# Pooled attention and a bilinear layer on one core: p times v for both heads per 128 queries, on two column halves of the array

## The chip, the core and the metric

The kernel runs on one core of one Trainium2 chip. Five engines work side by side, each with its own queue that it works off in order: TensorE (PE in the profile; its weight loads are listed apart as PEld), VectorE (DVE), ScalarE (ACT), GpSimd (POOL), and SyncE (SP), which here only issues DMAs. They wait for each other through semaphores. The metric is the device time of one execution in microseconds (us); the median of the runs counts.

## What is computed

```python
# attention: batch 4, heads 8, keys 1152, head dimension 64
q_pool = q.reshape(B, H, S // 2, 2, D).mean(axis=3)            # 576 queries
scores = scale * np.matmul(q_pool, k.transpose(0, 1, 3, 2))
scores = scores - np.max(scores, axis=-1, keepdims=True)
attn = np.exp(scores)
attn = attn / (np.sum(attn, axis=-1, keepdims=True) + 1e-09)
x = np.matmul(attn, v)                                         # 4 x 8 x 576 x 64
# bilinear layer on the 2304 tokens (512 wide, 1536 inside)
a = x @ w_a
b = x @ w_b
out = a * b @ w_out
```

Inputs and outputs are float32. To keep that precision with float16 products the kernel splits p, v, x and the weights w_a and w_b (and, from the second batch on, k and q) into a high and a low float16 part; a product is then three products: high times high, high times low, low times high.

## The kernel before, in words

**Attention.** Two heads form a pair; there are 16 pairs, four to a batch. A pair's 576 queries are worked in rows of 128 queries: two rows make the "even" token group (256 tokens), two the "odd" group (256), and 64 queries are the "rest". A block is 128 queries of one head, or the rest's 64 queries of both heads: nine blocks a pair, 144 in all. A block passes through: scores on PE into the PSUM tile `sps` (`qk`, and `qk_rest` for what didn't fit); the minimum of the negated scores on DVE (`sm_max`, L566), which also moves them to `s`; exp on ACT (L573); sum and reciprocal on DVE; the high part p on ACT (`sm_hi`, L586) and the low part on DVE (`sm_lo`, L590); and one DMA that transposes both parts into a slot of `pt` (`transpose`, L596, issued by SP).

**p times v.** `unit` (before) handles one head and all 256 or 320 queries of a token group at once, in the one PSUM bank `xps`. `pv` does it in two parts: nine matmuls (L622) whose weights are 128 columns, v's high and low part side by side, so that the upper 64 partitions collect v_hi p_hi and the lower 64 v_lo p_hi; then ten matmuls (L632) with v_hi alone (64 columns) and p_lo, which go in turn to the upper and the lower half. The two halves are then added on the way out: `x_copy` on ACT (L641) copies the upper half, `x_add` on DVE (L647) adds the lower. A pair takes four units and five of each of these. For each head the slots of `pt` that a unit reads must lie side by side, so each block has a fixed slot out of six.

**Weights and the bilinear layer.** The weights arrive as 64-bit pairs, 36 pieces of 512 KB; each is loaded into one of four `raw` buffers, in turn, and split there by ACT, DVE and POOL. The buffers are borrowed: two lie in `xt`, two in the lines 4 to 11 of `g`. The bilinear layer works in nine tiles of 256 tokens: `moe_mm` (L722, 288 matmuls a tile), `moe_a` on ACT and `moe_g` on DVE, and `moe_o` (L748, 72 matmuls a tile). Tile 0 needs the even tokens of all four pairs of batch 0 and the weights; the tiles 6, 8 and 7, which come last, need the last pair.

**What sets the order.** Every step is a task with a duration in us, a priority key and its buffers (`add`). The class `Plan` simulates the queues with the table `LAT` (latency from engine to engine), the DMA constants and PE's clock, tries 20 priority orders, and emits the best. So each number in the table or in an `add` can move any instruction on any queue. Once emitted, each engine's order is fixed.

Of the kernel before, what the change touches and what calls it, by code (L numbers as in the profile page):

```python
# [19 lines left out]
NQ = S // 2  # L20
# [10 lines left out]
A0, R0, REMN = (0, 64, 64, 64), (256, 0, 0, 0), 64  # L31
# [11 lines left out]
    (0.02, 0.29, 0.29, 0.29, 0.29),  # L43
    (0.3, 0.13, 0.14, 0.17, 0.17),
    (0.2, 0.14, 0.15, 0.17, 0.17),
    (0.15, 0.15, 0.15, 0.15, 0.15),
    (0.1, 0.0, 0.0, 0.0, 1.05),
)
SEED, TRIALS, SWEEPS = 3, 20, 3
DMA_START, DMA_END = 0.72, 0.97  # L50
Z_ALL = 30
W_KEY = (-3, 1.3)
W_PASSES = 4
PE_TICK, PE_WARM = 3.413, 1.275


class Plan:
# [9 lines left out]
    def add(self, eng, dur, key, fn, args=(), r=(), w=(), gen=0.45, block=0.0, port=None, lag=0.0, after=()):  # L67
# [14 lines left out]
        self.tasks.append((ENGINES.index(eng), dur, key, fn, args, sorted(deps), gen, block, eng == "POOL" if port is None else port, lag))  # L82
        return n

    def run(self, key, back):

        eng, dur, lat, out, left, gen, block, port, lag = self.back if back else self.forth
# [5 lines left out]
        dma_free = port_free = 0.0  # L93
        busy = {}
# [6 lines left out]
        for _ in range(n):  # L101
# [54 lines left out]
    def order(self):  # L156
        n = len(self.tasks)
        eng, dur, key, _, _, deps, gen, block, port, lag = map(list, zip(*self.tasks))
# [5 lines left out]
        self.forth = (eng, dur, LAT, out, [len(x) for x in deps], gen, block, port, lag)  # L164
        self.back = (eng, dur, back, deps, [len(x) for x in out], gen, [0.0] * n, port, lag)
# [22 lines left out]
def kernel(  # L188
# [53 lines left out]
    def PT(name, shape):  # L242
# [4 lines left out]
    xps = PT("xps", [128, 512])  # L247
    acc = [x.rearrange("p a n -> p (a n)") for x in ab]
# [8 lines left out]
        g_t[:, 4 * j:4 * j + 4].rearrange("p f n -> p (f n)").bitcast(I32).rearrange("p (n w) -> p n w", w=2)  # L257
        for j in (1, 2)
# [3 lines left out]
    z_t += [wab[:, NF - 1, m].rearrange("p a c n -> p (a c n)").bitcast(F32) for m in range(2)]  # L262

# [30 lines left out]
    def k_sum():  # L294

        nc.tensor.matmul(xps[:, 0:2], one.broadcast_to([128, 128]), kmx, start=True, stop=True)

    def k_scale(u):
        inv = ksc[:, u, 2:4]
        nc.vector.tensor_scalar(  # L300
            out=inv, in0=xps[:, 0:2], scalar1=2.0 ** -100, scalar2=2.0 ** -14, op0=ALU.max, op1=ALU.mult
# [30 lines left out]
    def prep_qk(ps_, key):  # L332
        n = ps_.q1 - ps_.q0
        if ps_.split:
            u = f"ksc{ps_.u}"
            add("SP", 2.5, key - 3, load_k, (ps_.p, 0), w=["kn0"])
            add("SP", 2.5 * n / NQ, key - 3, load_q, (ps_.p, ps_.q0, ps_.q1), w=["qraw"])
            add("POOL", 0.1 + 1.55 * n / NQ, key, q_sum, (0, n), r=["qraw"], w=["qs0"])
            add("DVE", 1.35, key, k_max, (), r=["kn0"], w=["kmx0"])
            add("DVE", 0.1 + 0.6 * n / NQ, key, q_max, (n,), r=["qs0"], w=["kmx1"])  # L340
            add("PE", 0.45, key - 2, k_sum, (), r=["kmx0", "kmx1", "ones"], w=["xps"])
            add("DVE", 0.7, key - 2, k_scale, (ps_.u,), r=["xps"], w=[u])
            return
# [154 lines left out]
    def prep_w(f, key):  # L498
        for m in range(3):
# [4 lines left out]
            if m < 2:  # L504
                add("DVE", 0.74, key, w_max, (f, m, n), w=[z, f"wmx{f}{m}"])
# [447 lines left out]
```

## Time and profile before

| | |
|---|---|
| median of 3 runs | 935.23 us (935.16 to 935.75) |
| profiled execution, its own time | 939.15 us |
| its span (first to last instruction) | 937.4 us |
| mean granted TensorE clock | 0.922 |
| PE, DVE, ACT, POOL busy | 85%, 76%, 64%, 28% of the span |
| DMA | 141.4 MB, 151 GB/s in the mean |

All rows come from the profiled execution. Shares of busy time are means over stages that differ much: the first sixth, in which the weights are prepared, a long middle, in which attention and the bilinear layer run side by side, and the last 170 us, in which only the bilinear layer is left. So the rows below are cut by stretch where that matters. A PE that is shown busy may run at either of two clock levels (granted clock 1.00 is 2.4 GHz, 0.50 is 1.2 GHz).

### The profile page before, as it was taken

The numbers are of one execution on the slowest core, as the hardware profiler recorded it, in microseconds if no ns is written. First come the engines' busy times: TensorE is split into PE (matmuls) and PEld (weight loads), VectorE is DVE, ScalarE is ACT, GpSimd is POOL, SyncE is SP. The second block draws the span as 40 slices with busy tenths as digits, with TensorE's granted clock in tenths as the row PEclk, the third lists the DMA queues.
The fourth block names the chain that finished last, engine by engine and source line by source line (L and its number), as shares of the span: only waits on it lengthen the run. The fifth ranks groups of instructions, "written<-read, shape, count | busy, mean of one in ns | idle before, by whom it ended". The sixth has DMA issues, their size and how long they took to land.

```text
span 937.4 us, 15587 instructions
## 1 busy us (share of the span) xinstructions
PE 792.7 (85%) x5856; PEld 562.4 (60%) x5856; DVE 710.0 (76%) x1352; ACT 600.6 (64%) x973; POOL 265.0 (28%) x228
## 2 busy tenths in 40 slices
PE   4546436998789988669999999899999998999997
PEld 2323224665456755337766776576677666877885
DVE  6699999996799889998999799989889873112010
ACT  5677977966577768857787687667867762232212
POOL 4547687622311012111023113201310231110303
PEclk9666667999789999969999999999999999999999
DMA  7999799886989889987878979979786674000100
GB/s 254 235 205 243 201 236 221 222 188 121 198 174 157 155 164 195 206 167 146 174 156 167 176 152 161 199 130 175 150 162 141 103 151 76 1 23 2 23 1 23
DMA packets 353644, 141.40 MB, mean 151 GB/s; under 512 B 338208, under 2 KB 340256, under 8 KB 353568
## 3 DMA queue, kind: packets, MB, share of 16 engines
q1 hardware_dynamic: 353568, 140.40, 71.5%
q8 instruction: 46, 0.75, 0.3%
q14 instruction: 30, 0.25, 0.1%
HBM read 50.72 MB, written 4.72 MB: 59 GB/s over the span
## 4 chain that ended last, share of the span: by engine, by line
PE 50%; DVE 8%; issue 3%; DMA 2%; ACT 2%; POOL 0%; ACTq 0%; DVEq 0%
PE ab L722 24%; PE ab L748 12%; PE sps L538 7%; PE xps L622 4%; DVE p L590 2%; PE xps L632 2%; DVE s L566 2%; DMA pt<-p 2%; ACT p L586 1%; ACT g L729 0%; DVE k L315 0%; DVE x L647 0%; DVE g L734 0%; DVE o L754 0%; ACT s L573 0%
## 5 line engine op out<-in xcount | busy, mean ns | idle before, releaser
L722 PEld LDWEIGHTS <-wab 128*128 128x128 f16 x2592 | 248.9, 98 | 42.6 <-issue 6.2
L722 PE MATMUL ab<-xt,wab 128*128 128x256 f16 x2304 | 267.0, 274 | 2.8 <-DVE o L754 1.6
L590 DVE SCALAR_TENSOR_TENSOR p<-s,st,p 128x1152 f16<-128x1152 f32 x144 | 212.8, 1484 | 9.9 <-ACT p L586 9.6
L573 ACT ACTIVATE s<-s,st 128x1152 f32<-128x1152 f32 x144 | 179.9, 1250 | 56.3 <-DVE s L566 55.4
L586 ACT ACTIVATE p<-s,st 128x1152 f16<-128x1152 f32 x144 | 178.2, 1245 | 22.1 <-DMA pt<-p 7.8
L742 POOL TENSOR_TENSOR gl<-g,gh 128x256 fp32r<-128x256 f32 x108 | 95.9, 892 | 308.6 <-ACT gh L739 299.2
L566 DVE TENSOR_SCALAR_CACHE_REDUCE s<-sps,ksc 128x1152 f32<-128x1152 f32 x108 | 152.8, 1414 | 20.6 <-PE sps L538 18.5
L748 PE MATMUL ab<-wo,gh 128*128 128x512 f32 x432 | 144.4, 416 | 4.9 <-DVE g L734 4.9
L538 PE MATMUL sps<-k,q 64*128 64x512 f16 (+3 forms) x1080 | 122.0, 339 | 29.9 <-DVE s L566 25.1
L729 ACT ACTIVATE g<-ab,cc 128x256 f32<-128x256 f32 (+1 forms) x144 | 56.0, 417 | 106.0 <-PE ab L722 105.7
L622 PE MATMUL xps<-pt,vs 128*128 128x256 f16 (+1 forms) x576 | 91.4, 310 | 37.0 <-DMA pt<-p 17.2
L538 PEld LDWEIGHTS <-q 64*128 64x128 f16 (+1 forms) x1080 | 58.6, 99 | 102.9 <-issue 63.2
L734 DVE SCALAR_TENSOR_TENSOR g<-ab,cc,g 128x256 f32<-128x256 f32 (+1 forms) x144 | 56.2, 412 | 75.3 <-ACT g L729 74.7
L535 PE MATMUL sps<-k,q 64*128 64x512 f32 (+3 forms) x240 | 71.4, 675 | 41.5 <-DVE s L566 33.4
L622 PEld LDWEIGHTS <-vs 128*128 128x128 f16 x576 | 58.3, 106 | 59.9 <-issue 39.4
L748 PEld LDWEIGHTS ab<-wo,gh 128*128 128x128 f32 x432 | 78.0, 192 | 26.5 <-DVE g L734 2.6
L748 PE MATMUL ab<-wo,gl 128*128 128x512 f32 x216 | 86.7, 402 | 0.0
L535 PEld LDWEIGHTS sps<-k,q 64*128 64x128 f32 (+1 forms) x240 | 33.2, 236 | 79.1 <-DVE s L566 37.0
L739 ACT ACTIVATE gh<-g 128x256 fp32r<-128x256 f32 x108 | 43.9, 411 | 52.0 <-PE ab L748 50.9
L286 POOL TENSOR_TENSOR q<-qraw 128x576 f32<-128x576 f32 (+2 forms) x20 | 30.6, 1532 | 134.6 <-DVE q L323 42.0
L641 ACT ACTIVATE x<-xps 64x256 f32<-64x256 f32 (+2 forms) x80 | 28.1, 351 | 59.6 <-PE xps L632 54.9
L566 DVE TENSOR_SCALAR_CACHE_REDUCE s<-sps 128x1152 f32<-128x1152 f32 x36 | 48.7, 1353 | 9.1 <-PE sps L535 8.6
(88 smaller groups left out, 812.1 us busy)
## 6 DMA issues: line engine op xcount, KB each, us to landing
vraw<-in_v_dram SPq DMA_DIRECT2D x19, 576.0 KB, 4.5
k<-in_k_dram SPq DMA_DIRECT2D x19, 576.0 KB, 4.7
qraw<-in_q_dram SPq DMA_DIRECT2D x12, 576.0 KB, 5.0
g<-in_w_ab_dram SPq DMA_DIRECT2D x12, 512.0 KB, 4.5
xt<-in_w_ab_dram SPq DMA_DIRECT2D x12, 512.0 KB, 4.5
out_dram<-o SPq DMA_DIRECT2D x16, 256.0 KB, 2.8
g<-in_w_out_dram SPq DMA_DIRECT2D x6, 512.0 KB, 4.8
xt<-in_w_out_dram SPq DMA_DIRECT2D x6, 512.0 KB, 4.3
```

The source lines that it names most:

```text
L535: nc.tensor.matmul(out, qs[jq][rows, queries], kn[jk][rows, keys], start=True, stop=True)
L538: nc.tensor.matmul(out, qf[rows, hq - 1, queries], kf[rows, hk - 1, keys], start=(hq, hk) == (1, 1), stop=(hq, hk) == (2, 1),)
L566: nc.vector.tensor_scalar(out=s_t[sbuf(i)], in0=sps[:, at:at + S], scalar1=-1.0 / 16.0 if u is None else ksc[:, u, 4:5], scalar2=None, op0 ...
L573: nc.scalar.activation(out=s, in_=s, func=AF.Exp, scale=-1.0, bias=t[:, 0:1], accum_out=t[:, 1:2])
L586: nc.scalar.activation(out=p_t[pbuf(i)][:, 0], in_=s_t[sbuf(i)], func=AF.Copy, scale=st_t[i % NST][:, 3:4])
L590: nc.vector.scalar_tensor_tensor(out=p[:, 1], in0=s, scalar=st_t[i % NST][:, 3:4], in1=p[:, 0], op0=ALU.mult, op1=ALU.subtract)
L622: nc.tensor.matmul(xps[:, 0:w], vs[:, c, e].rearrange("p a d -> p (a d)"), pt[:, 0, c, c0:c0 + w], start=(c == 0), stop=False,)
L722: nc.tensor.matmul(dst if t < 8 else dst.rearrange("p (b n) -> p b n", b=B), wab[:, f, 1 - m, a, c], moe_x(t, b, c), start=(n == 0), stop= ...
L729: nc.scalar.activation(out=g_t[:, f, c], in_=ab[j][:, 1, c], func=AF.Copy, scale=cc[:, b, f, 0:1])
L734: nc.vector.scalar_tensor_tensor(out=g, in0=ab[j][:, 0, c], scalar=cc[:, b, f, 1:2], in1=g, op0=ALU.mult, op1=ALU.mult)
L742: nc.gpsimd.tensor_tensor(out=gl_t[j], in0=g_t[:, f], in1=gh_t[j].bitcast(F32), op=ALU.subtract)
L748: nc.tensor.matmul(acc[u], g[:, us], wo[:, f, a], start=(first and n == 0), stop=(last and n == 2))
```

## The change

- `unit` now handles both heads of one row of 128 (or 64) queries. `pv` (L634 after) makes, for each of nine key chunks, three pairs of matmuls with 64-column weights: head 0 to the upper 64 partitions of `xps`, head 1 to the lower 64. That is 54 matmuls a unit and five units a pair. All three products of a head add up in the same place, so nothing has to be added afterwards: `x_add` is gone.
- Units of one token group write neighbouring columns of `xps`; one `x_copy` over 128 partitions (`leave`) then takes out the whole group. The small column sums (`sums`) move to the last two columns of the same bank.
- The slots of `pt` are used in turn by all blocks.
- The queries stand in the same order in every batch (`A0`, `R0` are gone).
- Two of the four `raw` buffers change places: the one in `g` lines 4 to 7 goes, and one in `wab`'s slab 10 is borrowed until piece 30; after that only the two in `xt` are used.
- Nearly all figures of the planner change (durations, latencies, DMA constants), and it gets a price for changing the kind of matmul (`PE_TURN`). So the whole order is planned anew.

```diff
-A0, R0, REMN = (0, 64, 64, 64), (256, 0, 0, 0), 64
+REMN = 64
...
-    (0.02, 0.29, 0.29, 0.29, 0.29),
...
+    (0.0, 0.22, 0.13, 0.3, 0.3),
...
-DMA_START, DMA_END = 0.72, 0.97
-Z_ALL = 30
-W_KEY = (-3, 1.3)
+DMA_START, DMA_END, LOAD_LAG = 0.72, 0.63, 0.8
+Z_ALL, R_ALL = 30, 30
+W_KEY = (4, 1.3)
 W_PASSES = 4
-PE_TICK, PE_WARM = 3.413, 1.275
+PE_TICK, PE_WARM, PE_TURN = 3.413, 1.275, 0.1
...
                 if e == PE:
+                    if mode[i] != last:
+                        d += PE_TURN
+                        last = mode[i]
+                    end = t + d
...
+    sums = xps[:, 510:512]
...
-        g_t[:, 4 * j:4 * j + 4].rearrange("p f n -> p (f n)").bitcast(I32).rearrange("p (n w) -> p n w", w=2)
-        for j in (1, 2)
+        x.bitcast(I32).rearrange("p (n w) -> p n w", w=2)
+        for x in (wab[:, NF - 2].rearrange("p m a c n -> p (m a c n)"), g_t[:, 8:12].rearrange("p f n -> p (f n)"))
...
+    def ri(n):
+        return n % NRAW if n < R_ALL else n % 2
...
-        nc.tensor.matmul(xps[:, 0:2], one.broadcast_to([128, 128]), kmx, start=True, stop=True)
+        nc.tensor.matmul(sums, one.broadcast_to([128, 128]), kmx, start=True, stop=True)
...
+            last += ["raw2"] if f == NF - 2 and m < 2 else []
...
-            add("PE", 1.55 if ps_.split else 1.93, i - 8, qk, (ps_, rows, ps_.jk, ps_.jq), r=r, w=["sps0", "sps1"])
+            add("PE", 1.52 if ps_.split else 1.92, i - 8, qk, (ps_, rows, ps_.jk, ps_.jq), r=r, w=["sps0", "sps1"], mode=1)
         else:
-            add("PE", 0.18 if ps_.split else 0.24, i - 9, qk_rest, (ps_, rows, ps_.jk, ps_.jq), r=r, w=["sps1"],
-                after=(ps_.last_max,))
+            add("PE", 0.19 if ps_.split else 0.26, i - 9, qk_rest, (ps_, rows, ps_.jk, ps_.jq), r=r, w=["sps1"],
+                after=(ps_.last_max,), mode=1)
...
-        add("SP", 2.75, i, transpose, (i,), r=[p + "h", p + "l"], w=[f"pt{slot}"], gen=0.62, block=1.02)
...
+        add("SP", 2.97, i, transpose, (i,), r=[p + "h", p + "l"], w=[f"pt{slot}"], gen=0.42, block=1.02)
+
+    def pv(runs, at, w):
         for c in range(NCH):
-            nc.tensor.matmul(
-                xps[:, 0:w],
-                vs[:, c, e].rearrange("p a d -> p (a d)"),
-                pt[:, 0, c, c0:c0 + w],
-                start=(c == 0),
-                stop=False,
-            )
-        parts = [(c, c % 2, 0, w) for c in range(NCH - 1)]
-        parts += [(NCH - 1, 0, 0, w // 2), (NCH - 1, 1, w // 2, w)]
-        for c, u, a, b in parts:
-            nc.tensor.matmul(
-                xps[half(u), a:b],
-                vs[:, c, e, 0],
-                pt[:, 1, c, c0 + a:c0 + b],
-                start=False,
-                stop=(c == NCH - 1),
-            )
-
-    def x_copy(e, j, at, x0, w):
-        nc.scalar.activation(
-            out=x32[j][half(e), x0:x0 + w], in_=xps[half(0), at:at + w], func=AF.Copy, scale=1.0 / P_SCALE
-        )
-
-    def x_add(e, j, at, x0, w):
-        x = x32[j][half(e), x0:x0 + w]
-        nc.vector.scalar_tensor_tensor(
-            out=x, in0=xps[half(1), at:at + w], scalar=1.0 / P_SCALE, in1=x, op0=ALU.mult, op1=ALU.add
-        )
-
-    def unit(ps_, e, c0, runs, key):
-
-        w = sum(n for _, n in runs)
+            for n, (hp, hv) in enumerate(((0, 0), (0, 1), (1, 0))):
+                for e, c0 in enumerate(runs):
+                    nc.tensor.matmul(
+                        xps[half(e), at:at + w],
+                        vs[:, c, e, hv],
+                        pt[:, hp, c, c0:c0 + w],
+                        start=(c == 0 and n == 0),
+                        stop=(c == NCH - 1 and n == 2),
+                    )
+
+    def x_copy(j, at, x0, w):
+        nc.scalar.activation(out=x32[j][:, x0:x0 + w], in_=xps[:, at:at + w], func=AF.Copy, scale=1.0 / P_SCALE)
+
+    def unit(slots, at, w, key):
+        runs = [128 * t for t in slots] if len(slots) > 1 else [128 * slots[0], 128 * slots[0] + w]
+        add("PE", 0.1 + 1.49 * w / 128, key - 9, pv, (runs, at, w), r=[f"pt{t}" for t in slots] + ["vsh", "vsl"],
+            w=["xps"], mode=2)
+
+    def leave(ps_, at, x0, w, key):
         j = ps_.jx
-        xs = lambda x0, n: [f"x32{j}{e}{c}" for c in range(x0 // 64, (x0 + n) // 64)]
-        add("PE", 0.155 + 2.16 * w / 384, key - 9, pv, (e, c0, w),
-            r=[f"pt{c}" for c in range(c0 // 128, -(-(c0 + w) // 128))] + ["vsh", "vsl"],
-            w=["xps"] + [x for run in runs for x in xs(*run)])
-        at, after = w, ()
-        for x0, n in reversed(runs):
-            at -= n
-            c = add("ACT", 0.1 + 0.38 * n / 384, key - 4, x_copy, (e, j, at, x0, n), r=["xps"], w=xs(x0, n), after=after)
-            after = (add("DVE", 0.1 + 0.46 * n / 384, key - 4, x_add, (e, j, at, x0, n), r=["xps"], w=xs(x0, n)), c)
+        add("ACT", 0.072 + 0.192 * w / 256, key - 4, x_copy, (j, at, x0, w), r=["xps"],
+            w=[f"x32{j}{c}" for c in range(x0 // 64, (x0 + w) // 64)])
...
-                add("PE", 1.308, key + m, moe_mm, (t, f, m, j), r=r, w=[f"acc{j}"])
-            add("ACT", 0.42 if t < 8 else 1.1, -1000, moe_a, (t, f, j), r=[f"acc{j}"] + scs, w=[f"g{f}"] + ([f"raw{1 + f // 4}"] if t == 0 and f >= 4 else []))
-            add("DVE", 0.42 if t < 8 else 1.0, -1000, moe_g, (t, f, j), r=[f"acc{j}"] + scs, w=[f"g{f}"])
+                add("PE", 1.311, key + m, moe_mm, (t, f, m, j), r=r, w=[f"acc{j}"])
+            add("ACT", 0.37 if t < 8 else 0.88, -1000, moe_a, (t, f, j), r=[f"acc{j}"] + scs, w=[f"g{f}"] + (["raw3"] if t == 0 and f >= 8 else []))
+            add("DVE", 0.4 if t < 8 else 0.8, -1000, moe_g, (t, f, j), r=[f"acc{j}"] + scs, w=[f"g{f}"])
...
-            ends = {"even": (A0[b], A0[b] + TOK), "odd": (min(R0[b], 320), NQ)}
-            self.q0 = min(ends[x][0] if x == "even" else R0[b] for x in parts)
-            self.q1 = max(ends[x][1] for x in parts)
-            even, odd, rest = A0[b] - self.q0, 320 - self.q0, R0[b] - self.q0
+            self.q0 = XE if "even" in parts else XR
+            self.q1 = NQ if "odd" in parts else XR
+            even, rest, odd = XE - self.q0, XR - self.q0, XO - self.q0
+            pair = lambda q: [(0, q, 128), (1, q, 128)]
             self.todo = []
             if "even" in parts:
                 self.todo += [
-                    ([(0, even, 128), (1, even + 128, 128)], (0, 5), [], ()),
-                    ([(0, even + 128, 128), (1, even, 128)], (1, 4),
-                     [(0, 0, [(XE, TOK)]), (1, 512, [(XE, TOK)])], ("even",)),
+                    (pair(even), (0, 128), [], ()),
+                    (pair(even + 128), (128, 128), [(0, XE, TOK)], ("even",)),
                 ]
             if "odd" in parts:
                 self.todo += [
-                    ([(0, rest, 64), (1, rest, 64)], (2,), [], ()),
-                    ([(0, odd, 128), (1, odd, 128)], (0, 3), [], ()),
-                    ([(0, odd + 128, 128), (1, odd + 128, 128)], (1, 4),
-                     [(0, 0, [(XO, TOK), (XR, REMN)]), (1, 320, [(XR, REMN + TOK)])], ("rest", "odd")),
+                    ([(0, rest, REMN), (1, rest, REMN)], (0, REMN), [], ()),
+                    (pair(odd), (REMN, 128), [], ()),
+                    (pair(odd + 128), (REMN + 128, 128), [(0, XR, REMN + TOK)], ("rest", "odd")),
...
-        for _, slots, _, _ in ps_.todo:
-            blocks.extend(Block(n, slot) for n, slot in enumerate(slots))
+        for rows, *_ in ps_.todo:
+            for n in range(2 if rows[0][2] == 128 else 1):
+                blocks.append(Block(n, len(blocks) % NR))
...
-        for r, (rows, slots, spans_, splits) in enumerate(ps_.todo):
-            for n, _ in enumerate(slots):
+        for r, (rows, (at, w), leaving, splits) in enumerate(ps_.todo):
+            slots = []
+            for n in range(2 if w == 128 else 1):
+                slots.append(blocks[i].slot)
...
-            for e, c0, runs in spans_:
-                unit(ps_, e, c0, runs, i - 1)
+            unit(slots, at, w, i - 1)
+            for span in leaving:
+                leave(ps_, *span, i - 1)
```

Three places of the order show what moves. First PE, at the first p times v of the program; `vs` holds v's parts, `pt` the transposed p. Before, the last two of the nine wide matmuls and the first of the narrow ones:

```order
L622 LDWEIGHTS vs
L622 MATMUL xps<-pt,vs 128x256
L622 LDWEIGHTS vs
L622 MATMUL xps<-pt,vs 128x256
L632 LDWEIGHTS vs
L632 MATMUL xps<-pt,vs 64x256
```

and after, the first of the 54:

```order
L634 LDWEIGHTS vs
L634 MATMUL xps<-pt,vs 64x128
L634 LDWEIGHTS vs
L634 MATMUL xps<-pt,vs 64x128
L634 LDWEIGHTS vs
L634 MATMUL xps<-pt,vs 64x128
```

A unit now has one shape of matmul, half as wide in its weights and half as long.

Second DVE, at the last row of scores but one; `s`, `st` and `p` are a block's scores, sums and parts, `x32` is what p times v gives. Before:

```order
L577 TENSOR_SCALAR st_80<-st_80 128x1
L583 RECIPROCAL st_80<-st_80 128x1
L647 SCALAR_TENSOR_TENSOR x32_66<-xps_103,x32_66 64x256
L590 SCALAR_TENSOR_TENSOR p2_83<-s2_77,st_80,p2_83 128x1152
L566 TENSOR_SCALAR s1_76,st_80<-sps_100,ksc_79 128x1152
L684 TENSOR_SCALAR xt1_64<-xt1_64,vsc_94 128x2x256
```

and after, at the same stage of the last pair:

```order
L674 TENSOR_SCALAR xt1_64<-xt1_64,vsc_94 128x2x256
L576 TENSOR_SCALAR s0_75,st_80<-sps_100,ksc_79 128x1152
L600 SCALAR_TENSOR_TENSOR p1_82<-s1_76,st_80,p1_82 128x1152
L600 SCALAR_TENSOR_TENSOR p2_83<-s2_77,st_80,p2_83 128x1152
L724 SCALAR_TENSOR_TENSOR g_84<-ab1_102,cc_99,g_84 128x256
L576 TENSOR_SCALAR s1_76,st_80<-sps_100,ksc_79 128x1152
```

The add that stood between two steps of the softmax (L647) has no counterpart.

Third PE at the last scores of the program (L538 before, L548 after; `xt` and `wab` are the operands of `moe_mm`). Before:

```order
L538 LDWEIGHTS q1_74
L538 MATMUL sps_100<-k1_69,q1_74 128x128
L722 LDWEIGHTS wab_61
L722 MATMUL ab0_101<-xt1_64,wab_61 128x256
L722 LDWEIGHTS wab_61
```

and after:

```order
L712 LDWEIGHTS wab_61
L712 MATMUL ab1_102<-xt1_64,wab_61 128x256
L548 LDWEIGHTS q1_74
L548 MATMUL sps_100<-k1_69,q1_74 128x128
L548 LDWEIGHTS q1_74
L548 MATMUL sps_100<-k1_69,q1_74 128x128
L548 LDWEIGHTS q1_74
L548 MATMUL sps_100<-k1_69,q1_74 128x128
L634 LDWEIGHTS vs_72
L634 MATMUL xps_103<-pt_67,vs_72 64x128
```

Before, these scores came ahead of 72 matmuls of tile 6, the next p times v behind those; after, all 288 of tile 6 stand ahead of the scores, and a p times v right behind.

## Rows read from the trace of the kernel before

**Rows 1.** Busy time (share of the span) and instructions of each engine.

```profile
PE 792.7 (85%) x5856; PEld 562.4 (60%) x5856; DVE 710.0 (76%) x1352; ACT 600.6 (64%) x973; POOL 265.0 (28%) x228
```

**Rows 2.** Four stretches: length, busy time and instructions by engine, granted clock, DMA share.

```profile
0.00:158.00 158.00, 82.26 (x337) 44.76 (x338) 137.16 (x274) 117.16 (x175) 98.02 (x55) 0.71 0.89 227
158.00:450.00 292.00, 248.72 (x1900) 169.22 (x1899) 259.44 (x478) 205.56 (x314) 70.03 (x62) 0.93 0.86 175
450.00:765.00 315.00, 305.46 (x2492) 217.85 (x2490) 277.83 (x507) 229.87 (x360) 67.41 (x73) 0.99 0.83 158
765.00:937.40 172.40, 156.24 (x1138) 130.54 (x1132) 35.59 (x94) 48.00 (x126) 29.58 (x39) 0.97 0.12 27
```

**Rows 3.** PE's waits in the whole span: us in total, times, longest.

```profile
PE sps L535 <- DVE s L566: 33.4, 18, 6.8
PE sps L538 <- DVE s L566: 25.1, 17, 4.1
PE xps L622 <- DMA pt<-p: 17.2, 6, 8.0
```

**Rows 4.** L647 by stretch: length, DVE busy time and instructions, clock, DMA share.

```profile
0.00:450.00 450.00, 15.99 (x40) 0.85 0.87 193
450.00:765.00 315.00, 14.87 (x37) 0.99 0.83 158
```

**Rows 5.** DVE's timeline around one add: start, us, engine, line.

```profile
518.67 0.43 DVE L647 SCALAR_TENSOR_TENSOR x<-xps,x 64x256 f32<-64x256 f32 x1
519.02 1.41 DVE L590 SCALAR_TENSOR_TENSOR p<-s,st,p 128x1152 f16<-128x1152 f32 x1
```

**Rows 6.** DVE's waits ahead of L647, in 0 to 150, 150 to 450, 450 to 765.

```profile
DVE x L647 <- ACT x L641: 6.3, 1, 6.3
...
DVE x L647 <- ACT x L641: 8.7, 6, 3.1
...
DVE x L647 <- ACT x L641: 0.5, 1, 0.5
```

**Rows 7.** ACT, L641 by shape: busy us, mean ns of one, idle before it.

```profile
L641 ACT ACTIVATE x<-xps 64x256 f32<-64x256 f32 x48 | 17.8, 371 | 27.3 <-PE xps L632 23.0 <-DVE x L647 2.6 <-issue 0.6
L641 ACT ACTIVATE x<-xps 64x320 f32<-64x320 f32 x16 | 6.9, 430 | 5.6 <-PE xps L632 5.2
L641 ACT ACTIVATE x<-xps 64x64 f32<-64x64 f32 x16 | 3.4, 212 | 26.7 <-PE xps L632 26.7
```

**Rows 8.** PE's timeline at two units, of 320 and of 256 queries.

```profile
697.11 1.39 PE L622 MATMUL xps<-pt,vs 128*128 128x320 f16 x9
698.43 0.80 PE L632 MATMUL xps<-pt,vs 128*64 128x320 f16 x10
699.16 0.34 PE L538 MATMUL sps<-k,q 64*128 64x128 f16 x3
...
755.16 1.16 PE L622 MATMUL xps<-pt,vs 128*128 128x256 f16 x9
756.24 0.68 PE L632 MATMUL xps<-pt,vs 128*64 128x256 f16 x10
756.86 0.50 PE L748 MATMUL ab<-wo,gh 128*128 128x512 f32 x1
```

**Rows 9.** PEld's timeline at 526.5: loads for matmuls of 128 columns on two quarters.

```profile
526.52 0.17 PEld L538 LDWEIGHTS <-q 64*64 64x64 f16 x4
```

**Rows 10.** PEld, two groups by shape: busy us, mean ns of one, idle before.

```profile
L632 PEld LDWEIGHTS <-vs 128*64 128x64 f16 x640 | 33.1, 118 | 21.2 <-issue 17.6
L538 PEld LDWEIGHTS <-q 64*64 64x64 f16 x216 | 10.5, 106 | 12.3 <-issue 4.7
```

**Rows 11.** PE's timeline at the first scores of the program.

```profile
7.94 4.18 PE L535 MATMUL sps<-k,q 64*128 64x512 f32 x10 [1.37 <-DMA k<-in_k_dram]
```

**Rows 12.** PE's timeline from the last scores to the next p times v.

```profile
768.60 0.32 PE L538 MATMUL sps<-k,q 64*128 64x128 f16 x3 [1.19 <-DVE s L566]
768.86 8.03 PE L722 MATMUL ab<-xt,wab 128*128 128x256 f16 x72
780.85 1.40 PE L622 MATMUL xps<-pt,vs 128*128 128x320 f16 x8 [3.96 <-DMA pt<-p]
```

**Rows 13.** The chain that ended last, its end: start, us, what.

```profile
914.95 17.08 PE ab L748 x72
```

**Rows 14.** PE's waits from 450 to 765: us in total, times, longest.

```profile
PE sps L538 <- DVE s L566: 6.1, 4, 4.1
```

More of the change, by code (lines that the diff above doesn't have):

```diff
@@ L65, in __init__, with add @@
         self.readers = {}
-    def add(self, eng, dur, key, fn, args=(), r=(), w=(), gen=0.45, block=0.0, port=None, lag=0.0, after=()):
+    def add(self, eng, dur, key, fn, args=(), r=(), w=(), gen=0.45, block=0.0, port=None, lag=0.0, after=(), mode=0):
         n = len(self.tasks)
@@ L363, in v_sum @@
         nc.tensor.matmul(
-            xps[:, 0:2], one.broadcast_to([128, 128]), vmx[:, p:p + 1].broadcast_to([128, 2]), start=True, stop=True
+            sums, one.broadcast_to([128, 128]), vmx[:, p:p + 1].broadcast_to([128, 2]), start=True, stop=True
         )
@@ L459, in w_sum @@
     def w_sum(f):
-        nc.tensor.matmul(xps[:, 0:2], one.broadcast_to([128, 128]), wal[:, f], start=True, stop=True)
+        nc.tensor.matmul(sums, one.broadcast_to([128, 128]), wal[:, f], start=True, stop=True)
     def w_scale(f):
         nc.vector.tensor_scalar(
-            out=wsc[:, 1, f], in0=xps[:, 0:2], scalar1=2.0 ** -100, scalar2=2.0 ** -14, op0=ALU.max, op1=ALU.mult
+            out=wsc[:, 1, f], in0=sums, scalar1=2.0 ** -100, scalar2=2.0 ** -14, op0=ALU.max, op1=ALU.mult
         )
@@ L611, in block @@
         s, t, p = f"s{sbuf(i)}", f"st{i % NST}", f"p{pbuf(i)}"
-        ps_.last_max = add("DVE", 1.43, i - 4, sm_max, (i, ps_.u if ps_.split else None), r=[f"sps{blocks[i].head}"] + [f"ksc{ps_.u}"] * ps_.split, w=[s, t + "m", t + "s", t + "t", t + "r"])
-        add("ACT", 1.44, i - 3, sm_exp, (i,), r=[t + "m"], w=[s, t + "s"])
-        add("DVE", 0.14, i - 5, sm_sum, (i,), r=[t + "s"], w=[t + "t"])
-        add("DVE", 0.16, i - 5, sm_rec, (i,), r=[t + "t"], w=[t + "r"])
-        add("ACT", 1.245, i - 3.5, sm_hi, (i,), r=[s, t + "r"], w=[p + "h"])
@@ new lines, in block @@
+        add("ACT", 1.245, i - 3, sm_exp, (i,), r=[t + "m"], w=[s, t + "s"])
+        add("DVE", 0.065, i - 5, sm_sum, (i,), r=[t + "s"], w=[t + "t"])
+        add("DVE", 0.075, i - 5, sm_rec, (i,), r=[t + "t"], w=[t + "r"])
+        add("ACT", 1.15, i - 3.5, sm_hi, (i,), r=[s, t + "r"], w=[p + "h"])
+        add("DVE", 1.37 if ps_.split else 1.4, i - 3, sm_lo, (i,), r=[s, p + "h", t + "r"], w=[p + "l"], port=True)
+        add("SP", 2.97, i, transpose, (i,), r=[p + "h", p + "l"], w=[f"pt{slot}"], gen=0.42, block=1.02)
@@ L698, in x_split @@
         name = {"even": f"x{b % 2}{c}0", "odd": f"x{b % 2}{c}1", "rest": f"xr{b}{c}"}
-        xs = [f"x32{j}{e}{m}" for e in range(2) for n in which for m in range(at[n][0] // 64, sum(at[n]) // 64)]
+        xs = [f"x32{j}{m}" for n in which for m in range(at[n][0] // 64, sum(at[n]) // 64)]
         n = sum(at[m][1] for m in which) / NQ
         names = [name[m] for m in which]
-        add("ACT", 0.1 * len(which) + 0.6 * n, key, x_hi, (p, j, which), r=xs, w=[x + "h" for x in names] + alias)
-        add("POOL", 0.1 * len(which) + 1.4 * n, key, x_lo, (p, j, which), r=xs + [x + "h" for x in names],
+        add("ACT", 0.06 * len(which) + 0.55 * n, key, x_hi, (p, j, which), r=xs, w=[x + "h" for x in names] + alias)
+        add("POOL", 0.2 * len(which) + 0.9 * n, key, x_lo, (p, j, which), r=xs + [x + "h" for x in names],
             w=[x + "l" for x in names] + alias)
```

114 lines of the change are left out of this document (57 added, 57 removed).

## The prediction

> **What bounds the kernel now.** I read the busy shares first, then the same by stretch, then who waits for whom, then single instructions.
>
> Over the whole span PE is the busiest engine with 792.7 us, DVE follows with 710.0 [rows 1]. Cut by stretch, this falls apart [rows 2]. Up to 158 us PE is busy for 82 of 158 us at a mean granted clock of 0.71, and DVE for 137. From 158 to 450 PE loses 43 of 292 us, DVE 33. From 450 to 765 PE is busy for 305.5 of 315 us at clock 0.99, while DVE idles for 37. Behind that only the bilinear layer is left, and PE has nobody beside it. So up to 450 the kernel goes at the pace of the chain in which DVE stands, and from 450 on at that of PE. What PE waits for says the same: 58.5 us are waits for `sm_max` (33.4 in the batch without split k and q, 25.1 behind it), 17.2 for the transposes [rows 3].
>
> From this follows the rule for the sum: work taken from DVE counts up to 450 and hardly behind it; work added to PE counts from 450 on and hardly before it.
>
> **The add that goes.** 80 adds (L647) go, 40 of them before 450 with 15.99 us of busy time and 37 before 765 with 14.87 [rows 4]. A record on DVE is longer than what it costs: the add at 518.67 lasts 0.43 us, but the next instruction starts 0.35 us after it [rows 5]. With that ratio, 0.35 / 0.43, the 40 early adds cost 13.0 us. I count these in full. The late ones, some 12 us, I count at nothing: PE's work covers them, and PE waits for only 9.5 of those 315 us [rows 2].
>
> **The waits that go with it.** DVE, which works in order, stands still ahead of the adds until ACT has copied, and ACT until PE has finished the unit: 6.3 us up to 150, 8.7 from 150 to 450, 0.5 up to 765 [rows 6]. Everything queued behind the add, `sm_max` above all, stands with it. After the change only ACT waits for the unit. The 15.0 us are an upper bound; the lower one is nothing, since PE itself may stand in front of the same unit, waiting for the transposes, and can't give DVE scores in that time (the wait of 8.0 us in rows 3 is of that kind). I take the middle, 7.5.
>
> **The copies.** 80 copies on ACT become 32 over all 128 partitions. That takes some 15 us from ACT: 17.8 + 6.9 + 3.4 = 28.1 now, then 16 of 0.371 and 16 of 0.430 if a row's length sets the time [rows 7]. ACT idles 36% of the span and is waited for less than DVE. I count nothing. The late copies are hidden behind PE; should they be late, the next unit waits on PE, since `xps` is one bank.
>
> **p times v on PE.** Today 320 queries of one head take from 697.11 to 699.16, 2.05 us, and 256 queries 1.70 [rows 8]. Nine wide matmuls of 320 columns start 0.136 us apart or less (1.32 us for nine with the change of kind behind them). The ten narrow ones take 0.73 with the change of kind behind them: alternating halves run side by side, or ten of that length would take 1.3. A pair costs 2 x (2.05 + 1.70) = 7.5 us. After: 27 couples a unit, 128 columns each. What a couple with two new 64-column weights takes, no row shows in that form. The nearest is the rest's scores, 128 columns on two quarters of the array: four loads end within 0.17 us, one lasts 0.106 [rows 9, 10], so the second two start about 0.06 behind the first two. With 0.056, 128 columns at 2.4 GHz and 3 ns of gap, a unit streams for 1.51 us, the 64-query unit for 0.80, a pair for 6.85 against 13.5 x 2 x (0.136 + 0.109) = 6.62 now: 0.23 more, 3.7 for 16 pairs. Changes of kind cost about 0.1 us each (the 2.05 us less 13.5 x 0.136, halved); in the two orders I count 361 and 340, 2.1 us less. In sum PE gets 1.6 us more, of which half is behind 450: plus 1.
>
> The bounds of this are wide. Below: couples can't beat the columns, so not under 1.44 us a unit. Above: if each load held up its half for its whole record, 0.118 us [rows 10], a couple would take that, and a unit 3.2 us. I take 0.056, because the row nearest in form has two loads within it.
>
> The Trainium skill says otherwise (TensorE: Matmul & The Clock Gate, section LDWEIGHTS: a load takes its columns divided by 1.2, in ns; and TensorEngine Tiling (Array Packing), section Restrictions: column tiling switches off the fast weight load). By this 64 columns are an estimated 53 ns, and if the two halves' loads take turns, a couple takes 107 ns and a unit 2.9 us; if they go side by side, nothing changes. The four loads of rows 9 within 0.17 us speak for side by side, but on quarters, not on halves.
>
> **The start.** PE's first scores begin at 7.94 and wait 1.37 us for k [rows 11], whose load is third on SP's queue behind v and q. In the new order q and k are the first two and v follows; the v work, which DVE did meanwhile, moves behind. I count 1 us, between 0 and 1.4.
>
> **The end.** The last scores start at 768.60, and the p times v that needs them at 780.85: 12.2 us for the last blocks to pass softmax and transpose. PE covers 8.0 of this with tile 6 and waits 3.96 [rows 12]. In the new order tile 6 stands ahead of the last scores; behind them come a unit, 18 matmuls of `moe_o` and the last unit. Such matmuls go at 17.08 / 72 = 0.237 us [rows 13]. That covers 0.3 + 1.7 + 18 x 0.237 = 6.3, so the wait becomes 5.9: plus 2.
>
> **Slots, raw buffers, order of the queries.** With slots in turn a block waits for the unit six blocks before it; nothing in rows 3 waits for a slot, so nothing is gained by itself. A unit needs one row of blocks now, and each transposed row is used sooner, which helps PE's 17.2 us of waits for transposes only as far as the order leaves room. The raw buffer in `wab` frees four lines of `g`, but gives only two buffers to the last six pieces of weights. Each of these may be worth some us either way; I count 0, with 5 on each side.
>
> **Sum.** -13.0 - 7.5 - 1.0 + 1.0 + 2.0 = -18.5 us. The profiled execution took 939.15 us for a span of 937.4; it would take 920.6. The median of the runs shown, 935.23, is 3.9 below the profiled one; the difference carries over: 916.7, so 917.
>
> **The rivals.**
>
> *The relief shows on both sides of 450.* All 15.0 of the waits go, and the late adds fill the 9.5 us that PE loses from 450 to 765: -13 - 15 - 1 - 9.5 + 1 = -37.5, 898. For it: DVE and PE are both over 88% busy there, and two engines at that level hold each other up in turn. Against: of those 9.5 us PE waited only 6.1 for `sm_max`, in four waits [rows 14]. Chance 15%.
>
> *The new order eats the gain.* The figures of the planner all change, and a plan that puts p times v right behind its transposes makes PE, which can't pass it, wait: 6 such waits cost 17.2 us before [rows 3], and there are 80 units in place of 64. If the early relief is turned into such waits, what stays is the start, the end and PE's extra: -1 + 2 + 1 to a few us below, 927 to 940. Against: the unit needs two blocks where it needed four or five. Chance 18%, a third of it within 0.2%.
>
> *The halves don't keep pace (slower).* If loads of 64 columns hold a couple up for 0.118 us, a unit takes 1.7 us more, a 64-query unit 2.4 more. Behind 450, where PE bounds, lie half of the units, 32 and 8: +73 us; with the early gain 935.2 - 20 + 73, about 988. It decides from the point at which 40 units cost more than the 20 us gained: 0.5 us each, a couple of 75 ns. For it: no row shows 54 such matmuls in a row, or as many instructions in so short a time; against it, rows 9. By the Trainium skill's figures above it would be an estimated 60 us in place of 73. Chance 12%. That the halves don't run side by side at all is the same case, and the ten narrow matmuls in 0.73 us speak against it [rows 8].
>
> **How the numbers follow.** Forecast 55% (907 to 927), relief on both sides 15% (895 to 907), gain eaten 18% (927 to 942), halves too slow 12%. Two points in ten may stay out, so the range runs from 897 to 940: it leaves out the slow halves and the outermost of the rest. A change of under 0.2% (1.9 us) can't be told from none in runs of this kernel. Faster by more than that: 55 + 15 + 5 = 75%; within it 6%; slower 12 + 7 = 19%.
>
> **What would show it.** In the new profile: a unit on PE in 1.5 to 1.75 us from its first matmul to the next kind (over 2.0 means that loads or issue hold it up). No DVE instruction waiting for `x_copy`. `sm_lo` of the 72nd block, the end of batch 1, some 15 to 20 us earlier. From there to the end about the same time as before, with PE over 95% busy. PE's waits for transposes no more than 17 us. What would make it wrong: PE idle as much before 450 as now (what it loses there would then be set by something other than DVE, by loads or POOL), or units that take over 2 us.

## The result: 892.4 us, and where the time went

The changed kernel takes 892.39 us in the median of 4 runs (889.51 to 894.62), the kernel before beside it 935.19; the ratio is 0.955, with a 95% interval of 0.9508 to 0.9592. I had forecast 917 and a range of 897 to 940. The direction was right; the gain was 43 us where I had 18, and the time lies below the range.

The profiled execution (894.62 us, span 892.8) by engine, to be read beside [rows 1]:

```profile
PE 778.5 (87%) x8960; PEld 589.0 (66%) x8960; DVE 669.3 (75%) x1272; ACT 583.9 (65%) x925; POOL 261.4 (29%) x228
```

DVE has 41 us less to do, ACT 17; PE's instructions are half as many again, its busy time 14 us less. The same stretches as in [rows 2], with the same columns:

```profile
0.00:158.00 158.00, 87.52 (x714) 56.42 (x715) 142.27 (x286) 124.12 (x186) 103.19 (x57) 0.73 0.97 244
158.00:450.00 292.00, 266.36 (x3581) 196.66 (x3580) 264.75 (x480) 218.48 (x323) 66.45 (x68) 0.98 0.98 191
450.00:765.00 315.00, 306.89 (x3827) 236.63 (x3827) 241.33 (x439) 205.94 (x318) 64.94 (x68) 0.99 0.76 143
765.00:892.80 127.80, 117.72 (x844) 99.27 (x842) 20.96 (x68) 35.31 (x103) 26.85 (x36) 0.97 0.07 18
```

Up to 450 both engines are busier than before, PE by 23 us, at a higher clock (0.98 for 0.93 in the second stretch), and DVE by 10. So with less to do, DVE idles less. The last matmul of tile 2 (the 864th of `moe_mm`) starts at 431.4 us, where it was 469.4: 38 of the 44.6 us by which the span is shorter are there already. PE has done the same work by then, an estimated 307 us at the full clock in both. The place is the one I had named, the size is not.

**Idle time and clock.** Of the 44.6 us, 30.4 are PE's idle time that is gone, 22.9 of them ahead of 450, and 14.2 are busy time. PE has no less to do, but less of it falls into stretches at the lower clock level (granted clock 0.5): summed over the traces, 66.0 us of PE's busy time for 97.4, of these 57.7 for 87.2 ahead of 450. Matmuls of one kind follow each other there at about twice the spacing (the wide ones of p times v, before, 208 ns for 110 in the mean). So an estimated 15.7 us, half of the difference and a third of the gain, come with the clock. My sum had no term for it.

**p times v.** PE's timeline at one unit after:

```profile
512.48 1.70 PE L634 MATMUL xps<-pt,vs 128*64 128x128 f16 x54
514.11 1.48 PE L712 MATMUL ab<-xt,wab 128*128 128x256 f16 x12
```

and its loads, in the timeline of PEld:

```profile
512.48 1.54 PEld L634 LDWEIGHTS <-vs 128*64 128x64 f16 x54
```

From the first matmul to the next kind it takes 1.63 us, of 40 such units behind 250 us in the median too; a couple follows a couple in 56 ns, and a load of either half is hidden in that. I had 1.51 and 0.1 to 0.2 for the changes of kind.

**DVE's waits.** DVE's waits up to 450 us (us in total, times, longest), first before, then after:

```profile
DVE x L647 <- ACT x L641: 14.9, 7, 6.3
DVE s L566 <- PE sps L535: 8.6, 8, 2.3
DVE s L566 <- PE sps L538: 6.9, 8, 1.5
```

```profile
DVE p L600 <- ACT p L596: 9.5, 11, 4.7
...
DVE s L576 <- PE sps L548: 5.5, 5, 2.7
...
DVE s L576 <- PE sps L545: 3.2, 3, 1.6
```

The waits ahead of the adds are gone, as they must be. But the waits for scores fell as well, from 15.5 to 8.7 us. No part of my sum had that; the experiments come back to it. PE, too, waited for the adds before, because they held `xps`; up to 450:

```profile
PE xps L622 <- DVE x L647: 8.3, 5, 5.9
```

That wait went with them, and my sum hadn't named it.

**Start and end.** PE's first scores after [rows 11] and its last ones [rows 12]:

```profile
5.98 4.18 PE L545 MATMUL sps<-k,q 64*128 64x512 f32 x10 [5.98 <-DMA k<-in_k_dram]
...
762.21 0.34 PE L548 MATMUL sps<-k,q 64*128 64x128 f16 x3
762.48 1.70 PE L634 MATMUL xps<-pt,vs 128*64 128x128 f16 x54
...
773.29 3.04 PE L634 MATMUL xps<-pt,vs 128*64 128x128 f16 x53 [4.55 <-DMA pt<-p]
```

The start is 2.0 us earlier (I had 1). At the end the last unit waits 4.55 us for its transposes, 0.6 more than before (I had 2 more).

**The signs.** Three of the signs I had named came as said: the unit's 1.63 us, PE busy for 95.9% of the time behind the 72nd `sm_lo`, and 15.8 us of waits for transposes. Two didn't: that `sm_lo` starts 26.7 us earlier (389.3 for 416.0) where I had 15 to 20, and the rest takes 17.9 us less where I had no change. So 27 of the 44.6 us lie ahead of this mark, which goes by softmax, and 38 ahead of the one above, at which PE's work is the same.

### The profile page after: what moved, and what is told of

The parts are those of the page before. It is cut to its first block, busy times and chain, and to the rows that moved or that the text cites. A ratio compares the mean times of both kernels' runs of the same rounds, so it can differ in the third digit from the quotient of the medians.

```text
span 892.8 us, 21607 instructions
## 1 busy us (share of the span) xinstructions
PE 778.5 (87%) x8960; PEld 589.0 (66%) x8960; DVE 669.3 (75%) x1272; ACT 583.9 (65%) x925; POOL 261.4 (29%) x228
## 4 chain that ended last, share of the span: by engine, by line
PE 38%; DVE 8%; DMA 3%; issue 3%; ACT 1%; POOL 0%; DVEq 0%; ACTq 0%; SPq 0%; POOLq 0%
PE ab L712 19%; PE ab L738 11%; PE sps L548 4%; PE xps L634 4%; DMA pt<-p 3%; DVE s L576 3%; DVE p L600 2%; DVE k L324 1%; DVE g L724 1%; DMA vraw<-in_v_dram 0%; DVE vmx L368 0%; ACT p L596 0%; DVE q L332 0%; POOL q L295 0%; DVE kmx L298 0%
## 5 line engine op out<-in xcount | busy, mean ns | idle before, releaser
L712 PE MATMUL ab<-xt,wab 128*128 128x256 f16 x2304 | 264.3, 273 | 0.2 <-DVE xt L674 0.2
L600 DVE SCALAR_TENSOR_TENSOR p<-s,st,p 128x1152 f16<-128x1152 f32 x144 | 209.6, 1467 | 20.0 <-ACT p L596 19.4
L634 PE MATMUL xps<-pt,vs 128*64 128x128 f16 (+1 forms) x4320 | 133.8, 221 | 21.6 <-DMA pt<-p 15.8
L634 PEld LDWEIGHTS <-vs 128*64 128x64 f16 x4320 | 121.7, 115 | 36.4 <-issue 31.4
L548 PE MATMUL sps<-k,q 64*128 64x512 f16 (+3 forms) x1080 | 119.8, 333 | 15.7 <-DVE s L576 11.4
L548 PEld LDWEIGHTS <-q 64*128 64x128 f16 (+1 forms) x1080 | 56.9, 98 | 84.1 <-issue 37.3
L545 PE MATMUL sps<-k,q 64*128 64x512 f32 (+3 forms) x240 | 69.2, 655 | 45.6 <-DVE s L576 36.1
L449 POOL TENSOR_SCALAR xt<-xt 128x512 f16<-128x512 f32 x22 | 55.0, 2501 | 37.1 <-ACT xt L445 36.1
L295 POOL TENSOR_TENSOR q<-qraw 128x576 f32<-128x576 f32 (+2 forms) x20 | 28.2, 1409 | 128.1 <-DVE st L587 67.6
```

The lines of the kernel that those rows point to most:

```text
L545: nc.tensor.matmul(out, qs[jq][rows, queries], kn[jk][rows, keys], start=True, stop=True)
L548: nc.tensor.matmul(out, qf[rows, hq - 1, queries], kf[rows, hk - 1, keys], start=(hq, hk) == (1, 1), stop=(hq, hk) == (2, 1),)
L600: nc.vector.scalar_tensor_tensor(out=p[:, 1], in0=s, scalar=st_t[i % NST][:, 3:4], in1=p[:, 0], op0=ALU.mult, op1=ALU.subtract)
L634: nc.tensor.matmul(xps[half(e), at:at + w], vs[:, c, e, hv], pt[:, hp, c, c0:c0 + w], start=(c == 0 and n == 0), stop=(c == NCH - 1 and n ...
L712: nc.tensor.matmul(dst if t < 8 else dst.rearrange("p (b n) -> p b n", b=B), wab[:, f, 1 - m, a, c], moe_x(t, b, c), start=(n == 0), stop= ...
```

## Experiments

### Structure and figures apart, each planned anew

The change has two parts: the new structure (p times v, slots, buffers, order of the queries) and the new figures of the planner. Either alone first, then the adds taken out of the old kernel and put back into the new, all with a plan of their own.

New structure, old figures:

```diff
-    (0.0, 0.22, 0.13, 0.3, 0.3),
+    (0.02, 0.29, 0.29, 0.29, 0.29),
...
-W_KEY = (4, 1.3)
+W_KEY = (-3, 1.3)
...
-        add("DVE", 0.065, i - 5, sm_sum, (i,), r=[t + "s"], w=[t + "t"])
+        add("DVE", 0.14, i - 5, sm_sum, (i,), r=[t + "s"], w=[t + "t"])
...
```

> The changed kernel with all the planner's figures as they were (latencies, durations, DMA constants, weights' key, no price for changing the kind of matmul); only the durations of the two steps that are new, p times v and the copy, are kept. Theory A (the exit of p times v: 80 adds and DVE's waits ahead of them go in full, not by half): most of the 43 us stay, 900 to 910. Theory B (the new figures make the better order): half or less stays, 915 to 925. Theory C (any new plan falls 10 us better or worse by chance): anything from 890 to 925, not to be told from the others by this run alone.

Measured: 921.56 us, ratio 0.9859 (0.9832 to 0.9887). A third of the gain; theory A's range is missed.

Old structure, new figures (the same lines the other way round, in the kernel before):

> The kernel before with all the planner's new figures (the two steps that go, copy and add, and p times v keep their old ones). Theory A: little, 925 to 937. Theory B: 910 to 920. Theory C: 920 to 945.

Measured: 938.88 us, ratio 1.0057 (1.0031 to 1.0083). Not a gain at all: theory B, in its plain form in which the figures bring the gain by themselves, falls. Theory A had most of the 43 us in the run before, which has a third, and falls as well.

The old kernel without its adds:

```diff
-            after = (add("DVE", 0.1 + 0.46 * n / 384, key - 4, x_add, (e, j, at, x0, n), r=["xps"], w=xs(x0, n)), c)
+            after = (c,)
```

> The kernel before without its 80 adds (v's and p's lower parts that sit in the other half of PSUM are left out of x), planned anew. PE's work and everything else stays. Theory A: the adds' 26 us and DVE's waits ahead of them go, 905 to 915. Theory B: only the share that I had predicted for this, 917 to 922, the rest of the 43 us needs the figures. Theory C: 905 to 930.

Measured: 929.04 us, ratio 0.9928 (0.9892 to 0.9965), worse than any theory's range but C's.

The new kernel with adds put back:

```diff
+        for e, a, b in cuts:
+            add("DVE", 0.06 + 0.288 * (b - a) / 256, key - 4, x_again, (j, e, at + a, x0 + a, b - a), r=["xps"],
+                w=[f"x32{j}{c}" for c in range((x0 + a) // 64, (x0 + b) // 64)])
```

> The changed kernel with five instructions per pair put back on DVE behind each copy, of the shapes of the old adds; each adds zero times xps to x, so it holds xps and x as the old add did. Theory A: 30 us or more come back, 918 to 930. Theory B: 905 to 912. Theory C: 895 to 925.

Measured: 913.34 us, ratio 0.977 (0.9744 to 0.9797): 21 us come back, in theory C's range alone. The same adds are worth 6 us in one kernel and 21 in the other; but each of these runs has a plan of its own, so this may be the luck of the plan.

### The luck of the plan

One number, the planner's seed, changes the order and nothing else.

```diff
-SEED, TRIALS, SWEEPS = 3, 20, 3
+SEED, TRIALS, SWEEPS = 4, 20, 3
```

> The changed kernel with another seed of the planner (4 in place of 3): the same work, figures and rules, another of the orders it may find. Theory C (a plan falls better or worse by chance, by some 10 us): 885 to 912, clearly off 892 or clearly off the seed of the next run. Theory D (figures and structure belong together: the new figures help only where p times v has its new form): 889 to 896, as seed 3.

> The same with seed 5. Theory C: another time again, 885 to 912. Theory D: 889 to 896.

> The kernel before with seed 4. Theory C: 920 to 945, off 935 by more than 5. Theory D: 931 to 939.

> The new structure with the old figures (as the first run of the first set, 921.6), seed 4. Theory C: 900 to 930, off 921.6 by more than 5. Theory D: 917 to 926.

Measured: 897.57, 906.44, 919.98 and 912.36 us. All four lie outside theory D's ranges. Theory C holds as far as that the seed alone moves a kernel by up to 15 us. Later runs filled the table (each ratio to the kernel before beside it, two to eight executions a cell):

> The kernel before with seed 5. Seeds 3 and 4 gave 935 and 920. If seed 3 was a plan worse than most: 912 to 928. If seed 4 was better than most: 929 to 942.

> The kernel before with the new figures, seed 4 (seed 3 gave 938.9; without the figures the seeds 3, 4 and 5 gave 934, 920 and 942). Theory D (the figures help only with the new p times v): 925 to 942. Theory B (the figures help by themselves, and seed 3 was unlucky): 900 to 920.

> The new structure with the old figures, seed 5 (seeds 3 and 4: 921.6 and 912.4). Theory D (figures and structure pay only together): 908 to 928, over the 906 of the changed kernel's own worst seed. Theory C (luck of the plan alone): as likely under 906 as over it.

> The old structure with the new figures, seed 5 (seeds 3 and 4: 938.9 and 925.0; with the old figures seed 5 gave 942). Theory D: 922 to 945. Theory C: anything from 900 to 945.

| | seed 3 | seed 4 | seed 5 | mean |
|---|---|---|---|---|
| before | 1 | 919.98 (0.986) | 942.35 (1.0113) | 0.999 |
| new figures alone | 938.88 (1.0057) | 924.99 (0.9897) | 930.68 (0.9951) | 0.997 |
| new structure alone | 921.56 (0.9859) | 912.36 (0.9779) | 916.26 (0.9814) | 0.982 |
| both: the change | 892.39 (0.955) | 897.57 (0.962) | 906.44 (0.9715) | 0.963 |

Of the later runs, seed 5 of the kernel before and seed 4 of the figures alone miss the nearest range by less than 0.4 us (942 and 925), theory B's 900 to 920 is missed, and the last two fit theory D without speaking against C.

By the means the structure is worth 1.7%, 16 us, close to the 18 that I forecast for all. The figures are worth 0.2% on the old structure and 1.9% on the new one. What is left of the 4.5%, about 0.9% or 8 us, is that seed 3 is the best of three for the changed kernel. The six plans with the new structure, with whichever figures, take 892 to 922 us, the six with the old one 920 to 942; only one pair overlaps (old, seed 4, 919.98, and new, seed 3, 921.56). That the figures need the new structure rests on three seeds a row with a spread of up to 2.5% in one of them; it is likely, not settled.

### The adds at a fixed order

To take the plan out of it, the order was computed as in the original, and the adds were changed only where it is emitted. Every other instruction stands where it stood on its engine; the traces show the same sequence on PE, DVE, ACT and POOL.

Old order, adds left out:

```diff
-            fn(*args)
+            if fn.__name__ != "x_add":
+                fn(*args)
```

> The kernel before in exactly its old order on every engine, with the 80 adds left out when the order is emitted (v's and p's lower parts that sit in the other half of PSUM are missing from x). No new plan, so no luck of the plan. My sum had 13.0 + 7.5 us for adds and waits: 911 to 917. If only the work counts: 918 to 924. If adds and waits count in full, 28 us and the late ones too: 898 to 908. If the adds were hardly on the path: 928 to 934.

Old order, work without the wait:

```diff
     def x_add(e, j, at, x0, w):
-        x = x32[j][half(e), x0:x0 + w]
-        nc.vector.scalar_tensor_tensor(
-            out=x, in0=xps[half(1), at:at + w], scalar=1.0 / P_SCALE, in1=x, op0=ALU.mult, op1=ALU.add
-        )
+        nc.vector.tensor_reduce(out=spare[half(e)], in_=s_t[sbuf(last_lo[0])][half(e), 0:w], axis=AX.X, op=ALU.max)
```

> The kernel before in its old order, each add replaced by a maximum over as many elements of s, which is there already: DVE has the work but not the wait for ACT and p times v (the lower halves are missing from x). My sum: only the 7.5 us of waits go, 924 to 930. If the waits count in full: 917 to 922. If they don't count, PE standing before the same unit: 933 to 937.

New order, adds put in:

```diff
     def x_copy(j, at, x0, w):
         nc.scalar.activation(out=x32[j][:, x0:x0 + w], in_=xps[:, at:at + w], func=AF.Copy, scale=1.0 / P_SCALE)
+        for e, a, b in [(0, 0, w), (1, 0, w)] if w == TOK else [(0, 0, REMN), (0, REMN, w), (1, 0, w)]:
+            x = x32[j][half(e), x0 + a:x0 + b]
+            nc.vector.scalar_tensor_tensor(
+                out=x, in0=xps[half(e), at + a:at + b], scalar=0.0, in1=x, op0=ALU.mult, op1=ALU.add
+            )
```

> The changed kernel in exactly its order, with five adds per pair (zero times xps, so x stays) put in where the copy is emitted. If the relief is what my sum says, 20 us come back: 908 to 916. If the adds and their waits count more where DVE bounds longer: 918 to 930. If they are hardly on the path: 892 to 900.

Measured: left out, 930.16 us against 933.61 (ratio 0.9973, 0.9946 to 0.9999); without the wait, 933.49 (1.0007, 0.9986 to 1.0028); put in, 913.91 against the changed kernel's 892.39 (ratios to before 0.9803, 0.9756 to 0.985, and 0.955). The first barely differs from nothing, the second is nothing, the third is 21.5 us by the times and 24 by the ratios.

The clock hides a part of the first. The ten runs without the adds had a mean granted clock of 0.916, the nineteen with them 0.923. Span times what the clock lacks to 1 gives 78 us for 72, so the 3.4 us may hold an estimated 9 us of relief at most, still under half of the 20.5.

DVE's waits up to 450 us with the adds left out of the old order, to be held against those of before above:

```profile
DVE s L567 <- PE sps L536: 20.1, 8, 6.6
DVE s L567 <- PE sps L539: 13.1, 14, 2.6
```

The 14.9 us ahead of the adds are gone, and the waits for scores have grown from 15.5 to 33.2: DVE comes earlier and waits for PE. By the trace PE is at the scores themselves in 20.6 of these 33 us (13.7 before), at p times v in 6.8, at the bilinear layer in 3.0, and waits for transposes in 2.7. The sizes are those of one pair of profiled executions, whose spans differ by 11.1 us, more than the medians do. With the work kept and only the wait gone it is the same (18.4 + 11.3 = 29.7 us):

```profile
DVE s L568 <- PE sps L537: 18.4, 8, 6.2
DVE s L568 <- PE sps L540: 11.3, 10, 4.4
```

In the new order with the adds put in there is hardly such a wait:

```profile
DVE x L646 <- ACT x L643: 6.6, 7, 1.7
...
DVE s L576 <- PE sps L545: 2.3, 5, 1.1
```

and the span grows by 12 us up to tile 2 (the 864th `moe_mm` at 443.3 for 431.4) and by 8 behind it; PE's idle time grows by 9.9 and 7.9 us there. The adds' own time on DVE, up to 450 and from there to 765:

```profile
0.00:450.00 450.00, 15.86 (x42) 0.89 0.93 204
450.00:765.00 315.00, 13.15 (x35) 1.00 0.80 152
```

### Which figures

On the new structure, the DMA figures back, or those of the engines:

```diff
-        add("SP", 2.97, i, transpose, (i,), r=[p + "h", p + "l"], w=[f"pt{slot}"], gen=0.42, block=1.02)
+        add("SP", 2.75, i, transpose, (i,), r=[p + "h", p + "l"], w=[f"pt{slot}"], gen=0.62, block=1.02)
...
```

> The changed kernel with the planner's DMA figures alone as they were (transposes 2.75 us apart where 2.97 is put now, loads 2.5 and 2.2, their start and end). Theory E (the new order is good because it knows how slowly transposes follow each other, and so lets PE wait less for them): 905 to 925, and PE's waits for pt in the first 450 us back from 8 us to over 15. Theory F (the durations of DVE and ACT make it): 890 to 905, waits as now.

```diff
-        add("ACT", 1.245, i - 3, sm_exp, (i,), r=[t + "m"], w=[s, t + "s"])
-        add("DVE", 0.065, i - 5, sm_sum, (i,), r=[t + "s"], w=[t + "t"])
-        add("DVE", 0.075, i - 5, sm_rec, (i,), r=[t + "t"], w=[t + "r"])
+        add("ACT", 1.44, i - 3, sm_exp, (i,), r=[t + "m"], w=[s, t + "s"])
+        add("DVE", 0.14, i - 5, sm_sum, (i,), r=[t + "s"], w=[t + "t"])
+        add("DVE", 0.16, i - 5, sm_rec, (i,), r=[t + "t"], w=[t + "r"])
...
```

> The changed kernel with the durations and latencies of PE, DVE, ACT and POOL as they were, DMA figures, key of the weights and price of a change of kind new. Theory E: 890 to 905. Theory F: 905 to 925.

Measured: 903.5 us (ratio 0.9668, 0.9606 to 0.9729) with the DMA figures back, inside what seeds do to the changed kernel; 911.98 us (0.9758, 0.9696 to 0.982) with the engines' back, outside of it and where the structure alone lies. PE's waits for transposes did not rise with the DMA figures back (5.9 us up to 450): theory E, for which the DMA figures count, falls; both times lie in theory F's ranges, with one plan each. With the engines' figures back DVE waits for scores again, 21.1 us up to 450:

```profile
DVE s L576 <- PE sps L548: 13.8, 11, 5.5
DVE s L576 <- PE sps L545: 7.3, 9, 1.7
```

The structure alone has 22.8 (seed 3), the figures alone 11.2. Over all the traces this wait is 15.5 to 28.6 us in the eight plans made with the old engine figures and 7.0 to 16.2 in the nine made with the new ones, so it goes with these figures: the old ones gave a block 1.43 + 0.14 + 0.16 + 1.4 = 3.13 us on DVE, the new ones 2.85. My reading is that a plan that takes DVE to be slower than it is puts the next scores later on PE than DVE is ready for them; it fits, but is not shown. Nor does this wait carry the time by itself: on the old structure the new figures bring it down to between 7.0 and 11.2 us in all three seeds and gain 0.2%.

### More trials of the planner

```diff
-SEED, TRIALS, SWEEPS = 3, 20, 3
+SEED, TRIALS, SWEEPS = 3, 150, 3
```

> The changed kernel, seed 3, with 150 priority orders tried in place of 20. If the planner's own ranking of orders holds on the chip: 880 to 892. If it doesn't, the luck of the plan is larger than what more trials find: 888 to 905.

Measured: 890.16 us, ratio 0.9525 (0.9483 to 0.9568). The fastest of all, but in both ranges, and the changed kernel's interval (0.9508 to 0.9592) overlaps it; more trials pay little.

## Why the prediction was wrong

**The failed step: what bounds the kernel, and with it the rule for the sum.** I took DVE's busy share up to 450 as "the pace of the chain in which DVE stands" and priced the early adds in full and their waits by half. At the old order that price is 3.4 us (0.1 to 5.0) in place of 20.5. The runs showed in its place that DVE, freed of the adds, waits for PE: 17.7 us more for scores, where 14.9 ahead of the adds went. [rows 2] showed both engines idle, 43 and 33 us of 292, and the trace has them idle at the same time for only 0.8. They idled in turn, which fits two queues that wait for each other, not one bound.

**The term that was missing: the new plan.** I gave the planner's figures no term; "each of these may be worth some us either way; I count 0, with 5 on each side" was said of slots, buffers and queries, and the figures stood only in a rival, as a danger. By the means of three seeds the structure with its own plan is worth 16 us, the figures on top some 18, seed 3 some 8. A new plan of the same work moves the time by more than the 18 us of the forecast: 920 to 942 for the kernel before under three seeds. A range for a change that replans everything had to hold that, about 10 us on each side of its own, and mine hadn't.

**A term put at nothing: the clock.** [rows 2] had granted clocks of 0.71 and 0.93 ahead of 450, and I gave them no term. An estimated 15.7 of the 44.6 us come with the clock; this is another cut through the same gain, not more of it. The kernel before has 90.8 to 116.0 us of PE's busy time at the lower level under its three seeds, the structure alone 71.8 to 88.5, the changed kernel 66.0 to 78.1. No run changes the clock alone, so it stays open how much of the gain it makes and how much of it follows from an order in which PE idles less.

**The adds and their waits, 20.5 us.** Put into the new order they cost 21.5 to 24. The agreement is partly chance: I had all of it before 450, but 12 us came there and 8 behind, where I had counted nothing, since PE would cover it. It didn't: PE's idle time behind tile 2 grew by 7.9 us. Why PE gives no cover there in the new order was not tried.

**What was right.** PE's extra for p times v: 1.63 us a unit, loads side by side on the two halves; PE's busy time less the clock's share grew by an estimated 1.5 us, where I had 1.6. By the Trainium skill's time for a load (TensorE: Matmul & The Clock Gate, section LDWEIGHTS) a unit would have been an estimated 2.9 us if the two halves' loads took turns. That they might was my addition; the 56 ns a couple rule it out for this shape. So the rival of the slow halves falls. The rival in which the relief shows on both sides of 450 was nearest in time (898), but its reason, the full waits and a PE that fills up behind 450, isn't what happened: 38 of 44.6 us lie ahead of 450, and from there to 765 PE still loses 8.1 of the 9.5 us. Start and end were right in sign and within 1.4 us. The rival in which the new order eats the gain had it the wrong way round: by the means, more than half of the gain comes with the figures and the seed, that is with the order.

**Open.** Halves, slots, raw buffers and the order of the queries were not run apart from each other, nor was the weights' key apart from the other figures; with the seed worth 10 us, each would have needed several plans. That the figures need the new structure is likely, not settled, and the clock's part in the gain is open.

## What to carry to other kernels

Before pricing work taken from a busy engine, ask what it would wait for next: leave the work out at the old order and see what it gives. Where two engines idle in turn, what one is spared can go into waits for the other, and the same removal was worth 3 us in the old order, 6 with a new plan and over 20 in the new kernel. Where a planner sets the order, measure a change over several seeds. Its durations can be taken start to start from a trace: a `sm_sum` after is a record of 0.147 us, but the next instruction starts 0.064 behind its start. Sum PE's busy time at each clock level before and after, since a new order can move it. Judge a replanned kernel's single time with the spread of its seeds in mind.

## What I had not expected of the hardware

TensorE takes 54 matmuls with 54 loads of their own in 1.63 us, 108 instructions at 15 ns each, one half's 4 ns behind the other's, without falling behind the 128 columns of each couple. And the kernel before, which varied by 0.6 us in its first three runs, ran from 928.76 to 938.67 us in 19: half a per cent on either side, where I had taken 0.2% for what can be told from none.
